# Paced loads, messages by SyncE while loads remain, and turns of queries, keys and w3 chunks on all rows of TensorE at once

## The chip, the cores and the metric

The kernel runs on one core of a Trainium2 chip. The metric is device time in microseconds (us) of one execution, lower is better. Each run is slow when it lies over 1.5% above the fastest of the same kernel, fast otherwise; fast runs are compared with fast runs. A core has five engines that each work through a program of their own: TensorE (PE in the profile; PEld is its weight loads), VectorE (DVE), ScalarE (ACT), GpSimd (POOL), SyncE (SP). They wait for each other through semaphores. A "q" behind a name (SPq, POOLq) is the engine's sequencer, which takes instructions in order and issues them.

## The reference

Block-sparse attention, then a gated feed-forward product, without a nonlinearity in it:

```python
# q, k, v: (4, 8, 768, 64); sampled_blocks: (24, 3)
scores = scale * np.matmul(q, k.transpose(0, 1, 3, 2))
scores = np.where(mask, scores, -1000000000.0)     # window, first and last block, sampled blocks
attn = softmax(scores)
attn_out = np.matmul(attn, v)                      # -> x: (3072, 512)
a = x @ w1; b = x @ w2                             # 512 x 1024
h = a * b @ w3                                     # 1024 x 1024
return h @ w_out                                   # 1024 x 512
```

The kernel first multiplies w3 by w_out (its "fold"), so that the last two products become one. To do that it needs w3 transposed; to compute scores it needs queries and keys transposed.

## The kernel before

A planner lays out the whole program ahead of time: every piece of work has an engine, a duration and what it depends on, and the program is emitted in the planned order. Most products contract over 128 rows and run as two halves of 64 rows, each in its own half of the array (a "lane"). Halves of different products run side by side, so that one lane fills the gaps of the other. Both halves of a product add into the same bank (a piece of the memory that TensorE writes), and the program lets the second start only when the first is done. That handshake is a "message": an empty instruction on SyncE or GpSimd, whichever the plan finds free, that waits for the first half's last matmul; the second half waits for it.

```python
def ordered(box, part, mm):
    if part == 0:
        box["upper"] = mm.ins
    elif "told" in box:
        tc.add_manual_dep(mm.ins, box.pop("told").name, SYNC, reason="this half may start")

def tell(box, eng):
    told = box["told"] = (nc.sync if eng == "SP" else nc.gpsimd).nop(nofuse=True).ins
    tc.add_manual_dep(told, box.pop("upper").name, SYNC, reason="the other half is done")
```

Turns on TensorE (transpositions as products with an identity) are made in halves too: 14 of queries or keys at six chunks, two at four (their other two chunks are turned on all rows already), and eight of w3 at eight chunks:

```python
def emit(part, lane, j):                       # in transposes(); fold_transpose() is alike
    c, rows = lo + j, HALF[lane]
    if part == 0 and j == 0:
        take_bank(box, "tp", [128, 1024], BF16)
    ordered(box, part, nc.tensor.transpose(
        box["p"][:, c * 128 + 64 * lane:c * 128 + 64 * lane + 64],
        nat_of[b, pr][rows, c].rearrange("p h d -> p (h d)"), ident[rows, rows]))
```

Queries and keys of batches 1 to 3 that are not turned on TensorE are turned by DMA, which SyncE issues in pairs:

```python
def turn(eng):                                 # in turned()
    t = QK[b, pr] = qkt.tile([128, 2, S], BF16, tag="qkt", name="qkt")
    for x in range(2):
        nc.sync.dma_start_transpose(out=t[:, x, :].rearrange("r (c p) -> r c p", c=C),
                                    in_=ns[x].rearrange("p c h d -> p (c h d)"))
```

All loads are issued by GpSimd, which also carries messages; a load is just that:

```python
def load(emit, us, deps=(), dur=0.7):
    op = plan.add(Op("POOL", dur, lambda eng: emit(), deps))
    op.dma = us
    return op
```

The softmax here doesn't subtract the row's maximum and nothing guards it: scores larger than these inputs give would overflow.

## Time and profile before

| | before |
|---|---|
| time, median of 3 runs | 253.03 us |
| span in the profile | 251.7 us |
| TensorE busy / idle in the span | 239.0 / 12.7 us |
| waits of TensorE for its own program ("issue" gaps, start to start), before 62 us / later | 5.96 / 0.85 us |
| idle from 70 to 240 us | 0.5 us |
| messages by SyncE / by GpSimd | 194 / 19 |

How to read it: TensorE is the bound, above all behind 70 us, and its only sizeable idle time is early. An "issue" gap (nothing in the profile ended it) is put down to the program's delivery because the six of 0.4 us or more behind 15 us all end at an instruction whose number is the same modulo 256, and the program comes in blocks of 256.

### The profile page before, as it was taken

How to read it: one execution, taken by the hardware profiler on the slowest of the kernel's cores; microseconds unless marked ns; L12 is line 12 of the kernel's file. 1: busy time of each engine (PE TensorE's matmuls, PEld its weight loads, DVE VectorE, ACT ScalarE, POOL GpSimd, SP SyncE). 2: the span in 40 equal slices, each digit the busy share in tenths (PEclk: the TensorE clock that was granted, in tenths of full speed). 3: DMA queues.
4: the chain of work that ended last, by engine and by line, in shares of the span. 5: the costliest groups of instructions: out<-in, count | busy, mean ns of one | idle time of the engine just before them, and what ended most of it. 6: DMA issues, size and time to landing. Idle time of an engine off the chain costs nothing.

```text
span 251.7 us, 10960 instructions
## 1 busy us (share of the span) xinstructions
PE 239.0 (95%) x4817; PEld 189.0 (75%) x4817; DVE 180.5 (72%) x311; ACT 180.1 (72%) x342; POOL 76.9 (31%) x116
## 2 busy tenths in 40 slices
PE   7889889699999999999999999999999999999994
PEld 3568767668878889788878788988898887666642
DVE  7752343497799987879888679878879787788331
ACT  6869677688899999889989898889999781000000
POOL 4934757794960400259165010000000000000000
PEclk9979999999999999999999999999999999999998
DMA  6999999999997950399999835001020031000044
GB/s 188 180 195 182 181 207 188 179 176 105 113 134 94 120 42 3 64 143 185 97 118 144 186 98 43 4 35 54 5 87 3 3 128 46 0 3 0 11 158 167
DMA packets 80082, 25.59 MB, mean 102 GB/s; under 512 B 70180, under 2 KB 75044, under 8 KB 80036
## 3 DMA queue, kind: packets, MB, share of 16 engines
q0 software_dynamic: 61968, 13.90, 60.9%
q1 hardware_dynamic: 18032, 11.01, 18.0%
q8 instruction: 37, 0.61, 1.0%
q14 instruction: 9, 0.07, 0.1%
q10 hardware_dynamic: 36, 0.00, 0.0%
HBM read 29.36 MB, written 6.29 MB: 142 GB/s over the span
## 4 chain that ended last, share of the span: by engine, by line
PE 91%; DMA 4%; issue 2%; POOL 1%; SPq 0%; ACT 0%
PE o L874 21%; PE pb L950 15%; PE po L950 15%; PE pa L950 15%; PE s L828 14%; PE wp L950 6%; DMA w<-in_moe_w_dram 3%; PE xp L920 2%; DMA raw<-in_k_dram 1%; PE w3p L963 1%; PE tp L715 1%; SPq L516 0%; POOL vn L649 0%; POOL w L682 0%; ACT ob L588 0%
## 5 line engine op out<-in xcount | busy, mean ns | idle before, releaser
L836 ACT ACTIVATE e<-s 128x512 bf16<-128x512 f32 x288 | 153.8, 613 | 24.3 <-PE s L828 20.7
L828 PE MATMUL s<-qkt 64*128 64x256 bf16 x576 | 94.8, 271 | 0.6 <-DVE qkt L588 0.6
L950 PE MATMUL pa<-x,w_sb 64*128 64x512 bf16 x384 | 87.3, 376 | 0.0
L950 PE MATMUL pb<-x,w_sb 64*128 64x512 bf16 x384 | 85.7, 376 | 0.2 <-SPq L608 0.2
L874 PE MATMUL o<-vt,e 64*128 64x65 bf16 x2304 | 79.7, 190 | 2.9 <-issue 1.9
L874 PEld LDWEIGHTS <-e 64*128 64x128 bf16 x2304 | 75.7, 94 | 6.5 <-issue 3.3
L842 DVE TENSOR_TENSOR e<-e,mask 128x1920 bf16<-128x1920 bf16 x60 | 69.0, 1151 | 7.5 <-ACT e L836 6.9
L950 PEld LDWEIGHTS <-w_sb 64*128 64x128 bf16 x768 | 59.1, 94 | 16.8 <-SPq L608 1.2
L950 PE MATMUL po<-wf_sb,h 64*128 64x512 bf16 (+1 forms) x400 | 65.0, 368 | 0.0
L828 PEld LDWEIGHTS <-qkt 64*128 64x128 bf16 x576 | 45.7, 94 | 8.3 <-DVE qkt L588 0.9
L1015 DVE TENSOR_TENSOR h<-pb,a 128x512 bf16<-128x512 f32 x48 | 33.0, 688 | 11.9 <-PE pb L950 8.6
L950 PEld LDWEIGHTS <-h 64*128 64x128 bf16 x400 | 30.0, 94 | 11.1 <-SPq L608 1.5
L950 PE MATMUL wp<-wo_sb,wt 64*128 64x512 bf16 x128 | 31.6, 377 | 0.0
L588 ACT COPY ob<-po 128x512 f32<-128x512 f32 x10 | 5.9, 588 | 31.4 <-PE po L950 31.2
L646 POOL DMA_DIRECT2D vt<-in_v_dram x16 | 13.0, 820 | 36.3 <-PE xp L920 17.1
L828 PE MATMUL s<-G,hot 64*128 64x256 bf16 x96 | 20.6, 282 | 0.5 <-issue 0.5
L905 DVE TENSOR_TENSOR xn<-o,rec 128x256 bf16<-128x256 f32 x48 | 19.7, 419 | 1.1
L902 DVE RECIPROCAL rec<-o 128x4 f32<-128x4 f32 x48 | 8.5, 179 | 16.6 <-PE o L874 15.6
L588 ACT CAST a<-pa 128x512 bf16<-128x512 f32 x23 | 13.7, 597 | 7.5 <-PE pa L950 7.4
L588 DVE CAST a<-pa 128x512 bf16<-128x512 f32 x25 | 17.2, 689 | 2.4 <-PE pa L950 1.9
L588 DVE COPY ob<-po 128x512 f32<-128x512 f32 (+1 forms) x15 | 9.7, 653 | 12.6 <-PE po L950 10.6
L760 POOL DMA_DIRECT2D nt<-in_q_dram x16 | 13.1, 821 | 14.3 <-PE s L828 8.6
(69 smaller groups left out, 183.8 us busy)
## 6 DMA issues: line engine op xcount, KB each, us to landing
out_dram<-ob SPq DMA_DIRECT2D x23, 256.0 KB, 2.1
w<-in_moe_w_dram POOLq DMA_DIRECT2D x8, 256.0 KB, 7.7
w_sb<-in_moe_w_dram POOLq DMA_DIRECT2D x8, 256.0 KB, 6.5
vn<-in_v_dram POOLq DMA_DIRECT2D x8, 192.0 KB, 7.9
nt<-in_q_dram POOLq DMA_DIRECT2D x16, 96.0 KB, 4.5
nt<-in_k_dram POOLq DMA_DIRECT2D x16, 96.0 KB, 5.0
vt<-in_v_dram POOLq DMA_DIRECT2D x16, 96.0 KB, 4.8
kn<-in_k_dram POOLq DMA_DIRECT2D x12, 96.0 KB, 7.3
```

What stands on the lines that cost most here:

```text
L588: (nc.scalar.copy if eng == "ACT" else nc.vector.tensor_copy)(dst, src)
L646: nc.gpsimd.dma_start(out=t[:, h, :, :D], in_=src[b][:, 2 * pr + h])
L760: nc.gpsimd.dma_start(out=n[:, :, h, :], in_=src[b][:, :, 2 * pr + h, :])
L828: nc.tensor.matmul(box["s"][:, k2 * QT:(k2 + 1) * QT], lhsT=hot[HALF[h], kc, :] if what else qk[HALF[h], 1, kc * 128:(kc + 1) * 128], rhs= ...
L836: nc.scalar.activation(E[key][:, g, :], box["s"], AF.Exp, scale=1.0 / 8.0)
L842: nc.vector.tensor_tensor(e, e, m.to_broadcast((128, 4, 4, 120)), op=ALU.mult)
L874: ordered(box, part, nc.tensor.matmul(box["p"][:, g, :], lhsT=E[es[kp]][HALF[lane], g, at:at + 128], rhs=VT[(4 * b + 2 * Q + i) % NV][HALF ...
L902: nc.vector.reciprocal(box["rec"], box["p"][:, :, D:])
L905: nc.vector.tensor_tensor(XN[key][:, 256 * Q:256 * Q + 256].rearrange("p (g d) -> p g d", g=4), box["p"][:, :, :D], box["rec"].to_broadcas ...
L920: ordered(box, part, nc.tensor.transpose(box["p"][:, c, at:at + 64], XN[b, t, qh][rows, 128 * c:128 * c + 128], ident[rows, rows]))
L950: ordered(box, part, nc.tensor.matmul(box["p"][:, :width], lhsT=lhsT[HALF[lane]], rhs=rhs[HALF[lane], cols], start=part == 0 and j == 0, s ...
L1015: nc.vector.tensor_tensor(h_of["h"][:, f, :], box["p"], a_of[f], op=ALU.mult)
```

## The change

Its intent, as far as the code tells: loads are held back so that only some 8 us of load is on its way at a time, which should let other traffic through, the instruction blocks among it. The turns run on all 128 rows at once, which halves their instruction count and needs no handshake. And while loads remain to be issued, every message goes by SyncE, because a GpSimd that waits for the pace of its loads cannot pass messages.

```diff
     def tell(box, eng):
-        told = box["told"] = (nc.sync if eng == "SP" else nc.gpsimd).nop(nofuse=True).ins
+        if "upper" not in box:
+            return
+        told = box["told"] = (nc.sync if eng == "SP" or left else nc.gpsimd).nop(nofuse=True).ins
@@
+    on_way, AHEAD, left = deque(), 8.0, []
+
     def load(emit, us, deps=(), dur=0.7):
-        op = plan.add(Op("POOL", dur, lambda eng: emit(), deps))
+        def issue(eng):
+            left.pop()
+            made = emit()
+            for dma in made:
+                ahead, behind = sum(t for _, t in on_way) + us / len(made), None
+                while on_way and ahead > AHEAD:
+                    behind, t = on_way.popleft()
+                    ahead -= t
+                if behind is not None:
+                    tc.add_manual_dep(dma.ins, behind.ins.name, SYNC, reason="few loads at a time")
+                on_way.append((dma, us / len(made)))
+        left.append(1)
+        op = plan.add(Op("POOL", dur, issue, deps))
@@ transposes()
         def emit(part, lane, j):
-            c, rows = lo + j, HALF[lane]
             if part == 0 and j == 0:
-                take_bank(box, "tp", [128, 1024], BF16)
-            ordered(box, part, nc.tensor.transpose(... [rows, c] ..., ident[rows, rows]))
+                for x in range(n):
+                    whole(0, 0, x)
@@ fold_transpose()
             if part == 0 and j == 0:
                 take_bank(box, "w3p", [128, NF, 128], BF16)
-            ordered(box, part, nc.tensor.transpose(... w3_sb[i][rows, ...], ident[rows, rows]))
+                for x in range(NF):
+                    nc.tensor.transpose(box["p"][:, x, :], w3_sb[i][:, x * 128:(x + 1) * 128], ident)
```

(Every load returns the DMAs that it made, and the output weights are loaded in four pieces instead of one.) The planner does not know of any of this: it still plans two halves for a turn and puts messages where it did; the emitted program differs from its plan.

## The prediction

> **What bounds the kernel now.** I read the page first, from the top down. TensorE's row:
>
> ```profile
> PE 239.0 (95%) x4817; PEld 189.0 (75%) x4817; DVE 180.5 (72%) x311; ACT 180.1 (72%) x342; POOL 76.9 (31%) x116
> PE   7889889699999999999999999999999999999994
> ```
>
> TensorE is busy for 95% of 251.7 us, and the digits show where it is not: the first nine slices, about 56 us. Then the stretches, in the view by windows (columns: stretch, its length, then busy time and count of PE, PEld, DVE, ACT, POOL, then clock, DMA share, GB/s):
>
> ```profile
> 0.00:60.00 60.00, 51.59 (x1116) 40.19 (x1116) 32.03 (x74) 45.19 (x86) 39.54 (x70) 0.97 1.44 185
> 70.00:150.00 80.00, 79.47 (x1757) 65.85 (x1756) 67.21 (x108) 73.04 (x143) 26.19 (x34) 1.00 1.05 109
> 150.00:240.00 90.00, 90.00 (x1630) 70.33 (x1627) 70.97 (x112) 52.51 (x100) 1.53 (x2) 1.00 0.13 35
> ```
>
> Up to 60 us TensorE idles 8.4 us beside a stream of loads at 185 GB/s. From 70 to 240 us it idles 0.5 us in 170: there TensorE sets the end, and a stall put into it is paid almost in full. The chain of waits, from 28 to 50 us, says what the early idle time is (start, length, what):
>
> ```profile
> 29.43 1.18 issue
> 36.43 0.87 issue
> 42.73 0.48 issue
> 47.63 2.06 issue
> ```
>
> "issue" means that nothing in the profile released TensorE. I counted its instructions (weight loads and matmuls alike) up to each of these gaps: they end at number 961, 1217, 1473 and 1729 (gaps of 1.36, 1.19, 0.75 and 2.25 us from start to start), then 0.40 at 2241 and 0.57 at 5825. All lie a multiple of 256 apart: TensorE waits for its own program. The page's queue list has that transfer:
>
> ```profile
> q8 instruction: 37, 0.61, 1.0%
> ```
>
> 37 packets of 16 KB, each 256 instructions. In the trace such a packet starts 1.9 to 4.3 us after TensorE enters a block in the loaded phase (mostly under 1.5 us after 80 us), takes 1 to 1.8 us, and the gap ends 1.5 us later: 5.2 to 6.7 us in all, while a block of early work lasts only 4 to 7 us. The loads themselves are not the early bound: the q and k tiles land 2 to 6 us before TensorE uses them at 25 to 33 us, and 8 to 10 us before at 50 to 69 us. Only the second w3 chunk, at 13.8 us, holds it up (1.5 us).
>
> Last, the handshakes. A product in two halves lets the second half start only when SyncE or GpSimd has passed a message. Two answers show who passes them and what else SyncE does:
>
> ```profile
> L608 SPq EVENT_SEMAPHORE  x194: 17/17/17, 6.9 to 246.5; - x194
> L608 POOLq EVENT_SEMAPHORE  x19: 17/17/17, 36.5 to 149.2; - x19
> L769 SPq DMA_TRANSPOSE qkt<-nt x16: 1210/1216/2022, 73.3 to 149.1; - x16
> ```
>
> 194 messages go by SyncE and 19 by GpSimd. SyncE also issues 16 DMA transposes, in eight pairs, and each holds it 1.2 us or more.
>
> **What the Trainium skill says.** "Runtime: NRT & Kernel Launch", section Instruction fetch mechanics: the program is streamed in 16 KiB blocks of 256 instructions by the sequencer's own DMA queue, mostly hidden, and TensorE's buffer holds 2048 instructions. The trace agrees on the blocks, not on the rest: six gaps, 6.5 us in sum, and a block is asked for only one block ahead. "DMA: Bandwidth & Descriptors", Queues, rings and completion order: an engine goes round its queues packet by packet. That fits a fetch that waits longer under load. "TensorEngine Tiling (Array Packing)", Key Properties: changing the tiling mode drains the array. In the trace, a 64-row weight load follows a 128x128 spare matmul 147 ns after its start, where 56 ns is the step between two such; the other way round 198 ns against 109. So about 90 ns a switch. "Perfetto Trace Analysis", DMA Instruction — HWDGE: the issuing sequencer is free only at the reported end. The trace agrees: a pair's second transpose, long ready, starts 0.12 us after the first ends.
>
> **The change part by part.** The built order of both programs shows that all matmuls but the turns keep their order (4501, equal one by one). What differs:
>
> 1. *Turns on all rows.* 312 half transposes become 156 whole ones: 312 TensorE instructions fewer, counting weight loads. Time: the halves took 7.8 us start to start without gaps over 100 ns (222 at some 32 ns, 81 woven into the other half's work at 10 ns). The wholes at the 56 ns step that the trace shows for a warm pair: 156 x 56 = 8.7 us. Switches: 24 items x 2 x 90 ns = 4.3 us at most. Sum +5.2 us; as some items lie side by side and the first seven fall where data is awaited anyhow, I count +4.
> 2. *Their handshakes.* 24 messages go. Gaps of 0.1 to 0.2 us ahead of second halves: 1.7 us by my count. -1.7.
> 3. *Instruction fetch.* With 312 fewer instructions before 70 us, block borders fall at other work. Placing them on before's timeline with its gaps taken out, the blocks last 6.4, 6.4, 6.1, 4.5, 6.1, 6.5 and 4.2 us where they lasted 6.2, 3.9, 6.7, 4.7, 5.7, 4.4 and 3.7. At some 6 us per fetch the short ones still stall, 2 to 3.5 us in sum where 5.95 were lost by 61 us. -3.
> 4. *Pacing.* The framework already keeps at most eight loads on their way (each issue waits for the eighth before). The new limit of 8 us of load binds for the 256 KB chunks (six of 1.27 us) and for the output weights, now in four pieces; runs of 96 KB pieces stay limited by the eight. The queue is first come, first served and never dry (loads land 5 to 13 us after issue), so landings don't move. It may shorten the fetch a little: 0 to -1, within the range.
> 5. *Messages moved.* While loads remain to be issued (the last at about 150 us), every message now goes by SyncE. All 19 of GpSimd lie before that. The first moved one of each cluster stands in SyncE's order just behind a pair of DMA transposes. The eight, with the start of the second half that needs it now, and the end of the pair:
>
> ```
> needed at   75.59  80.29  85.45  103.15  125.05  129.74  138.88  148.84
> pair ends   75.98  81.70  87.29  104.43  126.01  132.04  140.70  150.32
> stall (+.1)  0.5    1.5    1.9     1.4     1.1     2.4     1.9     1.6
> ```
>
> Sum 12.3 us. The pair starts right behind the message before it, as now, so it won't move ahead of TensorE. I take off 5% for work that catches up: +11.7.
>
> Sum: +4 - 1.7 - 3 + 11.7 = +11. From 253.0: 264; a little off for pacing gives **263.5 us**.
>
> **The rivals.** (a) *The early gain is all there is*: the moved messages come in time, the fetch gaps go, and the time is 247 to 250. For it: the gaps are real, and the author meant this. Against it: the eight pairs, whose ends lie behind the need in each case. It would hold if a transposing issue did not block SyncE. (b) *The stalls come but are made up*, because ScalarE gets ahead meanwhile: 255 to 259. Against it: from 70 us on TensorE has next to no idle time that a freer ScalarE could fill. (c) *Worse than the sum*: stalls of 2 us drop TensorE's clock. The gap at 12 to 13.8 us was followed by matmuls of 410 ns instead of 270, the one at 47.6 us by none: 266 to 270. (d) *Pacing starves the load stream*, and TensorE waits at 20 to 45 us: +1 to +4. Against it: six chunks, landing 1.25 us apart in the trace, cover 7.5 us, and the first load of all took 2.2 us from issue to landing.
>
> **Range and chances.** The stalls range from 9 (two missed, some made up) to 14 us (longer transposes); the early part from -4 to +3. So 257 to 269 holds it 8 times in 10. Faster by over 2% (under 248.0) needs (a) with all of the fetch gain: 0.04. Within 2% (to 258.1) needs (b) or a large early gain: 0.14. Slower: 0.82.
>
> **What would show it.** Right: messages on GpSimd gone; eight gaps of 0.5 to 2.4 us on TensorE between 73 and 155 us, put down to SyncE, each ending with a pair of transposes; PE idle time in that stretch near 12 us instead of 0.5; "issue" gaps before 61 us at 2 to 3.5 us; whole transposes at 56 ns; 60 us' worth of early work finishing within 2 us of before. Wrong: the stretch from 70 to 150 us as full as now (then SyncE is not held, or the messages are not needed there); or fetch gaps unchanged (then the count of instructions does not set them).

## The result, and the profile after

| | before | after |
|---|---|---|
| time, median (range), 4 runs each | 252.93 us (252.31 to 255.64) | 268.13 us (267.78 to 268.57) |
| span in the profile | 251.7 us | 266.4 us |
| TensorE busy / idle | 239.0 / 12.7 us | 249.5 / 16.9 us |
| "issue" gaps before 62 us / later | 5.96 / 0.85 us | 0 / 2.12 us |

The change made the kernel slower: ratio 1.058, 95% interval 1.050 to 1.066. (A ratio here is the mean time of one kernel's fast runs over that of the other's fast runs of the same rounds, so not quite the ratio of the medians.)

TensorE's row and slices on the page of the kernel after:

```profile
PE 249.5 (94%) x4661; PEld 190.5 (71%) x4661; DVE 181.4 (68%) x311; ACT 181.9 (68%) x342; POOL 78.7 (30%) x119
PE   8899999999987799899879698999999999999994
```

The idle slices have changed places: the early ones are full now, and there are 7s and a 6 in the middle. TensorE does more: 10.5 us more busy time with 156 matmuls fewer. The same three stretches as before, in the view by windows:

```profile
0.00:60.00 60.00, 58.13 (x1006) 42.16 (x1008) 32.97 (x77) 46.91 (x87) 43.52 (x76) 1.00 1.46 186
70.00:150.00 80.00, 71.01 (x1531) 57.30 (x1529) 62.02 (x98) 66.10 (x127) 26.11 (x33) 1.00 1.06 92
150.00:240.00 90.00, 87.57 (x1726) 70.82 (x1728) 68.79 (x110) 60.80 (x115) 0.00 (x0) 0.98 0.14 42
```

Up to 60 us TensorE is busy 58.1 us where it was 51.6, yet it has not got further: at equal points of the program (both programs hold the same 4501 matmuls besides the turns, in the same order) it is 0.95 us later at 72 us (a half of one lane may start a little before or after its neighbour of the other; the order within each lane is the same). So that busy time is not more work done. From 70 to 150 us it idles 9.0 us where it idled 0.5. The loads move 186 GB/s early, as before. The shares of the chain that ended last, before and then after:

```profile
PE 91%; DMA 4%; issue 2%; POOL 1%; SPq 0%; ACT 0%
```

```profile
PE 88%; SPq 4%; DMA 4%; issue 1%; ACT 1%; POOL 1%
```

SyncE's sequencer is new in it, with 4% of 266 us. One of its places in the chain of waits, from 82.67 us (start, length, what):

```profile
82.67 0.12 PE s L840
82.80 0.06 SPq L781
...
82.97 1.21 SPq L781
84.18 0.05 issue
84.23 0.02 SPq L610
84.25 0.05 issue
84.29 0.39 PE pa L962
```

L781 is the issue of a DMA transpose, L610 a message, L962 the second half of a feed-forward product. The data of that second half is not late: what it waits for is the message, the message stands behind a transpose that holds SyncE for 1.21 us, and 0.05 us after the transpose's end it is passed on. The answers on the two lines show the rest (count, then shortest, median and longest in ns, then first and last start), and that GpSimd passes no message any more:

```profile
L610 SPq EVENT_SEMAPHORE  x189: 17/17/17, 18.3 to 261.2; - x189
L781 SPq DMA_TRANSPOSE qkt<-nt x16: 1211/1228/1910, 74.3 to 162.3; - x16
```

The waits of TensorE for it, in the view of waits (us in sum, times, longest):

```profile
PEld L962 <- SPq L610: 10.4, 17, 2.1
PE o L886 <- SPq L610: 3.5, 2, 2.0
PE pa L962 <- SPq L610: 3.4, 3, 1.5
PE pb L962 <- SPq L610: 3.1, 2, 1.9
```

The three PE rows hold seven waits, 10.0 us. The eight places one by one: the gap between starts of matmuls, less the ordinary step there (up to 0.1 us), and how much further after lies behind before once it is past. At the fifth, no gap is ended by SyncE: TensorE waited 0.86 us for its own program at 131.7 us, just ahead of it, and what it lost there is put in brackets.

| pair of transposes ends at (us) | 77.6 | 84.2 | 91.4 | 110.0 | 132.7 | 139.1 | 151.1 | 163.5 | sum |
|---|---|---|---|---|---|---|---|---|---|
| stall that the prediction listed | 0.5 | 1.5 | 1.9 | 1.4 | 1.1 | 2.4 | 1.9 | 1.6 | 12.3 |
| gap on TensorE | 1.09 | 1.73 | 2.17 | 1.25 | (0.4) | 1.68 | 2.30 | 1.57 | 11.8 without the fifth |
| further behind at equal points | 1.12 | 1.68 | 1.75 | 1.22 | (0.41) | 1.75 | 2.29 | 1.39 | 11.6, 11.2 without it |

Between them, two late waits for the program, at 120.8 and 147.1 us, add 0.64 and 0.60 us, and 0.93 us is lost right behind the stall that ends at 151.2 us. There the granted clock (the share of its full clock that TensorE is allowed) was 0.50 from 151.8 us for 3.4 us, and a step between two products of one lane that took 0.21 us at 155.6 us took 0.43 us at 154.2 us. 0.95 + 11.61 + 0.64 + 0.60 + 0.93 = 14.7 us, the difference of the spans; it stays at 14.7 to the end: nothing is caught up.

What a turn costs is seen on the timeline of TensorE (start, length, then operation). Before, two turns in halves (tp and w3p) woven into the products of the other lane:

```profile
26.84 0.19 PE L874 MATMUL o<-vt,e 64*128 64x65 bf16 x1
26.87 0.19 PE L963 MATMUL w3p<-ident,w 64*128 64x64 bf16 x1
26.87 0.19 PE L874 MATMUL o<-vt,e 64*128 64x65 bf16 x1
26.90 0.19 PE L963 MATMUL w3p<-ident,w 64*128 64x64 bf16 x1
```

After, a whole turn between two products:

```profile
31.43 0.82 PE L962 MATMUL wp<-wo_sb,wt 64*128 64x512 bf16 x3
32.18 0.51 PE L735 MATMUL tp<-ident,qn 128*128 128x128 bf16 x6
32.62 0.39 PE L962 MATMUL wp<-wo_sb,wt 64*128 64x512 bf16 x1
```

Before, the half turn of w3 starts every 30 ns while the other lane goes on every 30 ns: it takes next to nothing from it. After, the six chunks take the whole array for 0.44 us (32.18 to 32.62). The trace has their starts 56 ns apart, so 6 x 56 = 0.34 us are the stream and 0.10 us the way back to halves; 0.31 us passed between the start of the last product ahead of them and theirs, where two such products start 0.22 us apart. So the way in and the way back took 0.09 + 0.10 us here.

### The profile page after: what moved, and what is told of

It is laid out like the page before. It is cut to its first block, busy times and chain, and to the rows that moved or that the text cites. A ratio compares the mean times of both kernels' runs of the same rounds, so it can differ in the third digit from the quotient of the medians.

```text
span 266.4 us, 10632 instructions
## 1 busy us (share of the span) xinstructions
PE 249.5 (94%) x4661; PEld 190.5 (71%) x4661; DVE 181.4 (68%) x311; ACT 181.9 (68%) x342; POOL 78.7 (30%) x119
## 4 chain that ended last, share of the span: by engine, by line
PE 88%; SPq 4%; DMA 4%; issue 1%; ACT 1%; POOL 1%
PE o L886 20%; PE pb L962 14%; PE pa L962 14%; PE s L840 14%; PE po L962 14%; PE wp L962 6%; SPq L781 4%; DMA w<-in_moe_w_dram 2%; PE tp L735 2%; PE w3p L975 2%; PE xp L932 2%; DMA raw<-in_k_dram 1%; ACT e L848 1%; SPq L516 0%; POOL vn L664 0%
## 5 line engine op out<-in xcount | busy, mean ns | idle before, releaser
L840 PE MATMUL s<-qkt 64*128 64x256 bf16 x576 | 93.5, 271 | 0.8 <-DVE qkt L588 0.7
L962 PE MATMUL pa<-x,w_sb 64*128 64x512 bf16 x384 | 87.2, 378 | 3.4 <-SPq L610 3.4
L962 PE MATMUL pb<-x,w_sb 64*128 64x512 bf16 x384 | 85.9, 379 | 3.1 <-SPq L610 3.1
L886 PE MATMUL o<-vt,e 64*128 64x65 bf16 x2304 | 81.1, 190 | 4.9 <-SPq L610 3.5
L854 DVE TENSOR_TENSOR e<-e,mask 128x1920 bf16<-128x1920 bf16 x60 | 69.1, 1151 | 12.7 <-ACT e L848 12.4
L962 PEld LDWEIGHTS <-w_sb 64*128 64x128 bf16 x768 | 59.3, 94 | 25.5 <-SPq L610 8.4
L962 PE MATMUL po<-wf_sb,h 64*128 64x512 bf16 (+1 forms) x400 | 66.5, 370 | 0.0
L840 PEld LDWEIGHTS <-qkt 64*128 64x128 bf16 x576 | 44.3, 94 | 10.5 <-DVE qkt L588 1.8
L1025 DVE TENSOR_TENSOR h<-pb,a 128x512 bf16<-128x512 f32 x48 | 33.1, 689 | 16.0 <-PE pb L962 12.7
L962 PEld LDWEIGHTS <-h 64*128 64x128 bf16 x400 | 30.1, 94 | 9.6 <-SPq L610 1.2
L962 PE MATMUL wp<-wo_sb,wt 64*128 64x512 bf16 x128 | 32.1, 378 | 0.1
L840 PE MATMUL s<-G,hot 64*128 64x256 bf16 x96 | 19.3, 269 | 0.0
L588 DVE COPY ob<-po 128x512 f32<-128x512 f32 (+1 forms) x15 | 9.7, 653 | 12.6 <-PE po L962 10.6
```

The costliest lines, as they stand in the source:

```text
L588: (nc.scalar.copy if eng == "ACT" else nc.vector.tensor_copy)(dst, src)
L840: nc.tensor.matmul(box["s"][:, k2 * QT:(k2 + 1) * QT], lhsT=hot[HALF[h], kc, :] if what else qk[HALF[h], 1, kc * 128:(kc + 1) * 128], rhs= ...
L854: nc.vector.tensor_tensor(e, e, m.to_broadcast((128, 4, 4, 120)), op=ALU.mult)
L886: ordered(box, part, nc.tensor.matmul(box["p"][:, g, :], lhsT=E[es[kp]][HALF[lane], g, at:at + 128], rhs=VT[(4 * b + 2 * Q + i) % NV][HALF ...
L962: ordered(box, part, nc.tensor.matmul(box["p"][:, :width], lhsT=lhsT[HALF[lane]], rhs=rhs[HALF[lane], cols], start=part == 0 and j == 0, s ...
L1025: nc.vector.tensor_tensor(h_of["h"][:, f, :], box["p"], a_of[f], op=ALU.mult)
```

## The experiments

The change has three parts that can be had alone: pacing (P), whole turns (W), messages by SyncE (S). All kernels below gave correct results. Chips and calls differ by up to 1% in the time of the kernel before (medians 252.9 to 255.8 us), so each ratio is against the kernel before on its own chip. This table sums up the parts; busy and idle are TensorE's, from the page of each.

| kernel | parts | ratio (95%) | span | busy | idle | "issue" gaps before 62 us / later |
|---|---|---|---|---|---|---|
| before | - | 1 | 251.7 | 239.0 | 12.7 | 5.96 / 0.85 |
| pace_only | P | 0.998 (0.993 to 1.003) | 252.7 | 240.8 | 11.9 | 4.09 / 2.07 |
| whole_only | W | 1.006 (1.001 to 1.012) | 255.1 | 246.3 | 8.8 | 0 / 0.69 |
| planned_msgs | P W | 1.005 (1.000 to 1.011) | 256.2 | 245.6 | 10.6 | 0 / 2.02 |
| sp_alone | S | 1.031 (1.024 to 1.039) | 262.8 | 239.9 | 22.9 | 6.51 / 0.28 |
| whole_sp | W S | 1.057 (1.048 to 1.065) | 265.9 | 249.0 | 16.9 | 0 / 1.34 |
| after | P W S | 1.058 (1.050 to 1.066) | 266.4 | 249.5 | 16.9 | 0 / 2.12 |

**planned_msgs: the change, with messages as planned.** The theory was that moved messages carry nearly all of the loss; the rival, that whole turns or pacing cost something of that size themselves.

```diff
-        told = box["told"] = (nc.sync if eng == "SP" or left else nc.gpsimd).nop(nofuse=True).ins
+        told = box["told"] = (nc.sync if eng == "SP" else nc.gpsimd).nop(nofuse=True).ins
```

> The changed kernel, but the messages between halves go by SyncE or GpSimd as the plan has them (19 by GpSimd again). Theory A (the moved messages wait behind pairs of DMA transposes): the eight stalls of 0.4 to 2.3 us, 11.6 us in sum at equal places of the program, go, and 255 to 257 us are left. Theory B (the whole turns, with their changes of tiling mode, cost the time): it stays at 264 us or more. Theory C (paced loads come too late): it stays too, with waits on loads.

Measured: 257.38 us (256.74 to 257.92) against 255.82, ratio 1.005: just above the 255 to 257 us expected of the theory, and far from the rivals' 264. The stretch from 70 to 150 us of this kernel:

```profile
70.00:150.00 80.00, 76.07 (x1695) 63.60 (x1693) 64.93 (x104) 70.52 (x136) 24.54 (x31) 1.00 1.01 101
```

TensorE is busy for 76.1 us of it, against 71.0 with all parts; the gaps of the table above are gone. What is left are two waits for SyncE of 1.03 and 1.59 us, behind transposes that took 2.3 to 2.6 us in this run, and late waits for the program. So the moved messages are 10.2 us of span (266.4 to 256.2). The rest of the change is 4.5 us by the spans of two profiles from different chips, but half a per cent (1.3 us) by the ratio, which compares on one chip. The spans of the kernel before lie between 252.1 and 254.9 us in this call, so the size of the rest is known no better than that.

**sp_alone: the kernel before, with all messages by SyncE.** This is the suspected part alone, without anything that the rest could contribute.

```diff
-        told = box["told"] = (nc.sync if eng == "SP" else nc.gpsimd).nop(nofuse=True).ins
+        told = box["told"] = nc.sync.nop(nofuse=True).ins
```

> The kernel before with one edit: all messages by SyncE. Theory A: 264 to 266 us, with eight gaps of TensorE that end with a pair of transposes, 11 to 12 us in sum. Theories B and C: 252.5 to 254 us, as turns and loads are those of before.

Measured: 264.64 us (261.93 to 266.16) against 255.82, ratio 1.031. The same stretch:

```profile
70.00:150.00 80.00, 71.51 (x1571) 57.85 (x1566) 61.80 (x98) 65.93 (x127) 28.45 (x36) 1.00 1.21 100
```

8.5 us idle, as in the kernel after. The eight gaps are there: 0.52, 1.31, 2.54, 1.21, 1.32, 1.65, 1.68 and 1.57 us, 11.8 in sum, and at equal points this kernel falls 11.1 us behind the kernel before, as its span does. By its times it lost only 8.8 us; the kernel before was some 3 us slower than usual on that chip, and nothing that I ran tells why the two did not move together. The stalls are caused by the messages on SyncE alone, in either reading.

**pace_only: the kernel before, with the pacing.** Turns in halves, messages as planned.

```diff
 # the kernel after, with both turns as in the kernel before, and
-        ... (nc.sync if eng == "SP" or left else nc.gpsimd) ...
+        ... (nc.sync if eng == "SP" else nc.gpsimd) ...
```

> The kernel before with the loads paced and nothing else (turns in halves, messages as planned). If pacing shortens the instruction fetch by itself: gaps marked issue before 61 us under 2 us instead of 5.95, and 247 to 250 us. If the smaller count of instructions closed those gaps: 4 us of them or more stay, and 252 to 254 us. Theory C: waits on loads appear and 254 us or more.

Measured: 255.25 us (254.46 to 256.03) against 255.82, ratio 0.998. The early waits for the program fall from 5.96 to 4.09 us, and later ones rise from 0.85 to 2.07 us. The loads move 184 GB/s in the first 60 us, against 185. Eight us of load ahead is enough to keep the stream as full as before, and no gain shows. The 4 us that are left are what was expected if pacing by itself does not shorten the fetch.

**whole_only: whole turns without a limit on loads.** Messages as planned.

```diff
-    on_way, AHEAD, left = deque(), 8.0, []
+    on_way, AHEAD, left = deque(), 1e9, []
```

> The kernel before with the turns on all rows alone (no limit on loads, though the output weights come in four pieces; messages as planned). By my sum the turns cost 4 us and give back 1.7 of handshakes and 3 of fetch: 252 to 254 us. From the changed kernel's trace (1 us behind at 72 us with no fetch gap left) the turns cost 8 to 9 rather than 4: then 255 to 259 us, depending on the fetch gaps that stay without pacing. Theory B: 264 us or more.

Measured: 257.02 us (256.68 to 258.96), ratio 1.006. No wait for the program before 62 us. Its row on the page:

```profile
PE 246.3 (97%) x4661; PEld 190.1 (75%) x4661; DVE 181.0 (71%) x311; ACT 180.9 (71%) x342; POOL 79.0 (31%) x119
```

TensorE is busy 7.3 us longer than before (246.3 to 239.0) and idle 3.9 us less. Here the two sides of the early part can be read: the fetch waits are gone, and in their place the array is occupied for some 7 us more, as the second of the two expectations had it. At equal points it is 1.2 us behind at 72 us.

**touch: only the switch of modes.** One whole transpose of the item's first chunk ahead of each of the 24 half items, overwritten by the halves. It measures the disputed cost, that of leaving the half mode and coming back to it, while halves and handshakes stay. It also adds 48 instructions, where the change takes 312 away.

```diff
                 take_bank(box, "tp", [128, 1024], BF16)
+                nc.tensor.transpose(box["p"][:, lo * 128:lo * 128 + 128],
+                                    nat_of[b, pr][:, lo].rearrange("p h d -> p (h d)"), ident)
             ordered(box, part, nc.tensor.transpose(
@@ and in fold_transpose() before its halves
+                nc.tensor.transpose(box["p"][:, 0, :], w3_sb[i][:, :128], ident)
```

> The kernel before, with one whole-array transpose (its result is overwritten) put ahead of each of the 24 half-turn items: 24 x 56 ns = 1.3 us of streaming, and the same 48 changes of tiling mode that the whole turns bring. Theory D (a change of mode empties both halves of the array: some 0.26 us an item, as I read it from the changed kernel's trace): TensorE is 6 to 8 us later at 72 us than in the kernel before, and the time 2 to 3% longer. Theory E (the changes of mode are cheap; the whole turns cost because the halves were woven into other work for nothing): under 2.5 us later, within 1%.

Measured: 257.5 us (256.68 to 258.71) against 253.67, ratio 1.016. Its row on the page:

```profile
PE 248.6 (98%) x4841; PEld 194.0 (76%) x4841; DVE 181.3 (71%) x311; ACT 181.2 (71%) x342; POOL 77.2 (30%) x116
```

9.6 us more busy time than before, for 24 chunks that stream in 24 x 56 ns = 1.3 us. The other 8.3 us are 0.35 us an item: an estimate, since busy spans are partly modelled. Counted otherwise, as 2.9 us further behind plus 5.25 us of vanished fetch waits less the stream, it is 0.29 us. Neither theory's range was met: 3 us later at 72 us and 1.6% lie between D and E; it is with the vanished waits added that D's cost comes out. Both counts take in all else that differs between the two executions: behind its wait at 13.8 us the kernel before ran at a granted clock of 0.50 from 14.9 us for 3.4 us, and touch did not. A third count leaves that out: how much further behind touch is right after a visit than right before it. For the twelve visits behind 20 us that lie clear of before's fetch waits the median is 0.29 us with the stream, or 0.23 us without. So a visit of the whole array among halves costs 0.2 to 0.35 us besides its stream, by estimate.

The surprise is the waits for the program: 0.71 us of 5.96 are left, though this program is longer than before. So the waits do not vanish because there are fewer instructions. What fits is that TensorE waits when the work of a block lasts less than its successor takes to come. The trace has the packets of that transfer, so both can be read (a block counted from where TensorE enters it, waits included; a fetch to the landing of the packet, plus the 1.5 us after which the waits ended):

| blocks entered between 25 and 57 us | 1 | 2 | 3 | 4 | 5 | 6 |
|---|---|---|---|---|---|---|
| before: block / fetch, us | 5.2 / 5.2 | 6.7 / 6.7 | 5.9 / 5.9 | 6.5 / 6.4 | 6.7 / 5.8 | 4.0 / 4.0 |
| touch: block / fetch, us | 4.7 / 4.8 | 6.8 / 7.0 | 4.8 / 3.7 | 5.7 / 3.4 | 6.6 / 5.7 | 4.8 / 4.5 |

In before, five of six blocks last just as long as the fetch. In touch, longer work is one half of the story (without its wait of 2.25 us, before's fourth block is 4.2 us of work, against 5.7); the other is that two fetches came 2.2 and 3.0 us sooner, for which no run has the cause. Fetch waits and added work fill the same time: of the 9.6 us of added busy time here, idle time gave 6.5 (12.7 to 6.2 us), and the span grew by 3.1.

**w3_whole_pace: a smaller share of whole turns.** Pacing, and only the eight turns of w3 whole, which have eight chunks per switch; messages as planned. If the fetch gain and the switches could be had in a better proportion, this would be a version that beats before.

```diff
 # the kernel after, with messages as planned and, in transposes(),
-                for x in range(n):
-                    whole(0, 0, x)
+            # ... the halves of the kernel before
```

> Paced loads (8 us), the eight w3 items whole, queries and keys in halves, messages as planned. With some 0.26 us a change-over and 8 x 8 x 56 ns the eight items should cost 3 us more than in halves; 128 instructions fewer should close two of the early fetch gaps, about 2 us. So within 1% of paced loads alone (ratio 0.99 to 1.01 to the kernel before). Were the changes of mode cheap: 0.98 to 0.99.

Measured: 254.58 us (252.66 to 256.34), ratio 1.005 (0.995 to 1.015). It is 1.46 us ahead of before at 72 us, and 0.11 us ahead at the end, by a wait of 1.36 us behind a transpose and later waits for the program. No gain that the rounds can see, as the expectation had it.

**pace5 and pace4: the pace tightened to 5 and to 4 us of load.** Halves, messages as planned. This asked where pacing begins to starve TensorE, and whether a thinner stream lets the program through.

```diff
-    on_way, AHEAD, left = deque(), 8.0, []
+    on_way, AHEAD, left = deque(), 5.0, []      # 4.0 in pace4
```

> Paced loads alone, but 5 us of load on their way instead of 8 (turns in halves, messages as planned). If the fetch waits behind the loads in flight, its early gaps fall below the 4.1 us seen with 8 us, to 1 to 3 us, and the time to 250.5 to 254 us on a chip where the kernel before takes 255.8 (ratio 0.98 to 0.995). If loads come too late: waits on loads appear and the ratio is over 1.00.

> As the run with 5 us, with 4 us on their way: three chunks of 256 KB. Fetch gaps under 1.5 us if they follow the loads in flight; but three chunks cover under 4 us of a path that takes over 2 us from issue to landing, so the load stream may show holes, and TensorE waits on loads before 45 us. Ratio 0.98 to 1.02, no more than a guess.

Measured: pace5 268.9 us, ratio 1.057 (1.047 to 1.067); pace4 280.3 us, ratio 1.106 (1.099 to 1.113). In pace5 the second of the expected cases came, loads too late and a ratio over 1.00; for pace4 the guess of 0.98 to 1.02 missed. Of the five early waits for the program, four are gone in pace5; the fifth, 0.41 us at 60 us in before, is 1.39 us and comes at 70 us, as this kernel is late by then. And the stream of loads falls to 152 GB/s in the first 60 us (138 in pace4). The view of waits of pace5, longest first among TensorE's:

```profile
PE o L889 <- POOLq L610: 7.4, 1, 7.4
...
PE pa L965 <- POOLq L610: 2.1, 1, 2.1
```

One wait of 7.4 us for a message on GpSimd. The chain of waits in that stretch shows what GpSimd was at:

```profile
39.23 3.83 DMA w_sb<-in_moe_w_dram
43.06 1.57 issue
44.63 1.47 POOL kn L667 x2
46.10 0.48 issue
46.58 0.02 POOLq L610
```

The message (L610) stands behind loads that wait for an earlier load to land. That is what the change moved its messages to SyncE for: the rule in it cures a fault of the pacing, one that at 8 us of load did not show.

**pace5_early_sp: the same, with messages by SyncE only until the first DMA transpose.** If that reading is right, the stall goes without a new one behind transposes.

```diff
+    turns = []                                  # turn() appends to it
-        ... (nc.sync if eng == "SP" else nc.gpsimd) ...
+        ... (nc.sync if eng == "SP" or not turns else nc.gpsimd) ...
```

> The kernel with halves and loads paced at 5 us, but messages go by SyncE until the first pair of DMA transposes has been issued (about 73 us), and as planned after it. Theory (messages on GpSimd stand behind loads that wait for their pace, and that is why the change sent them by SyncE): the stall of 7.6 us at 47 us, ended by a message on GpSimd, is gone; the waits on q and k loads at 27 to 34 us (3.9 us in sum) and the stall of 2.2 us at 87 us stay: ratio 1.02 to 1.035, some 7 us under the kernel paced at 5. Rival (the pace itself starves TensorE, and the message only happens to end the wait): the same stall is ended by a load instead, ratio 1.045 or more.

Measured: 269.64 us (266.58 to 271.04) against 255.36, ratio 1.064 (1.055 to 1.073). The total went against me (1.02 to 1.035 was expected). Its waits:

```profile
PE pa L966 <- POOLq L610: 6.8, 1, 6.8
PE tp L730 <- DMA qn<-in_q_dram: 4.1, 3, 2.5
PE w3p L979 <- DMA w<-in_moe_w_dram: 1.8, 2, 1.6
```

The stall at 47 us is gone, and at equal points the gain is what was foretold: at 74 us this kernel is 3.1 us behind before, where pace5 is 9.9 us behind. TensorE still waits on loads in that stretch, but the waits for its program, 5.55 us in before by 50 us, are gone, and at 50 us this kernel is 1.3 us ahead of before. The total missed its range because the same stall comes back. Once messages go by GpSimd again, one waits 7.0 us behind paced loads (to 85.7 us; 2.2 us at this place in pace5), and behind it another 1.4 us is lost while the granted clock is 0.50 (from 81.5 us for 6.8 us). The rival has a smaller share: the 3.1 us, or 4.5 us against pace_only, which is 1.4 us ahead of before there, are what the pace of 5 us costs by itself. Neither defect shows at 8 us.

**pace7_early_sp and pace7_again: the attempt at a version that beats both.** The same with 7 us of load ahead, run twice because most of its times were called slow.

```diff
-    on_way, AHEAD, left, turns = deque(), 5.0, [], []
+    on_way, AHEAD, left, turns = deque(), 7.0, [], []
```

> The same with 7 us of load ahead: a version that could beat both, if a shorter queue of loads lets the instruction fetch come sooner without starving TensorE. For that: fetch gaps before 62 us under 3 us (pacing at 8 us left 4.1 of 6.0), no load waits over 0.5 us, ratio 0.985 to 0.995. Against it (pacing moves only the fetch's luck): ratio 0.995 to 1.01, and gaps in another place.

> The same kernel again (halves, loads paced at 7 us, messages by SyncE until the first pair of DMA transposes), in more rounds, because three of its four times were called slow and one was 251.15 us. If it is a version that beats both, its ratio is under 0.99 with the interval below 1. If the one fast time was chance, the ratio is 0.995 to 1.005 and the interval holds 1.

Measured: 255.3 us (251.15 to 257.84, one fast run of four, so no ratio), then 256.55 us (251.38 to 258.77, two fast of six), ratio of the fast ones 0.994 (0.986 to 1.002). The profiles fell in the slow state; both show the waits for the program as they were (5.5 and 6.9 us before 62 us). The interval holds 1 and the medians are no better: not a gain that can be claimed. No version that I ran is clear of the kernel before.

**whole_sp: the change without its pacing.** Whole turns and messages by SyncE; the last corner of the table.

```diff
-    on_way, AHEAD, left = deque(), 8.0, []
+    on_way, AHEAD, left = deque(), 1e9, []
```

> The change without its pacing: whole turns, and all messages by SyncE while loads remain; the output weights still come in four pieces, as in the other kernels without the change's limit. Theory (the pace at 8 us moves nothing; stalls behind DMA transposes and the cost of mode switches make the difference): ratio 1.05 to 1.066, as the whole change, with the eight stalls of 10.5 to 12.5 us in sum. Rival (part of the 15 us comes from loads that are held back): ratio 1.03 to 1.045.

Measured: 267.3 us (266.34 to 269.25) against 254.24, ratio 1.057 (1.048 to 1.065), with seven gaps ended by SyncE of 11.6 us in sum. Two of its waits, to set beside those of the kernel after:

```profile
PE o L886 <- SPq L610: 3.2, 2, 1.9
PE pa L962 <- SPq L610: 3.5, 3, 1.4
```

As expected; the pacing has no part in the loss that these intervals can see. Here too the fifth pair has no gap of its own, and a stretch of 3.4 us at a granted clock of 0.50 follows a stall, at 92.6 us.

## Why the prediction was right or wrong

The time was foretold at 263.5 us and is 268.1, inside the range but near its upper end; the direction and the main cause were right. Step by step:

- *Messages moved, +11.7.* Right in cause and in size: seven of the eight stalls came, listed at 11.2 us in sum and found at 11.8 as gaps, 11.2 as distance that is lost. The eighth, listed at 1.1, was taken up by a wait for the program that cost 0.41. The 5% taken off for catching up was wrong in reason: nothing was caught up. sp_alone shows the cause by itself, planned_msgs its absence. The sign "idle time near 12 us" between 73 and 155 us reads 10.2, as the last stall falls at 163 us.
- *Turns on all rows, +4, and handshakes, -1.7.* The net of the two was +2.3 and is about +7: by busy time in whole_only 7.3 us, by distance 0.95 us behind at 72 us plus the 5.96 us of fetch waits that vanished = 6.9 us. (Both are low by some 1.0 us, which before alone lost at half clock from 14.9 us on.) The step of 56 ns was right. The switches, put at 2 x 90 ns an item, are 0.19 us in the example above and 0.2 to 0.35 us in touch, so they were mis-sized by a factor of two at most. More lies in the halves, counted as 7.8 us of TensorE's time: woven into the other lane they took less than their own stream. The distance before and behind the whole turns says so too: in whole_only the twelve items behind 20 us that lie clear of before's fetch waits cost 0.55 us more than their halves in the median, about the whole stream (six chunks, 0.34 us) and a visit.
- *Instruction fetch, -3.* It was -6 early, and some +1.3 later (2.12 us behind 62 us instead of 0.85). The prediction set lengths of blocks by instruction count against "some 6 us per fetch", and both were off. Its lengths in before are misread for four of seven blocks: with the waits taken out the trace gives 6.2, 3.8, 5.5, 5.2, 4.2, 6.7 and 3.6 us (the same sum). In the kernel after, the blocks entered from 25 to 54 us lasted 7.9, 5.4, 6.8, 8.0 and 5.5 us, as the whole turns in them took longer than counted, and the fetches 5.4, 3.5, 4.5, 5.8 and 3.4. touch, with 48 instructions more than before, has 0.71 us of early waits left, so their count does not decide. A part of the early gain is the turns' own slowness, and the terms for turns and fetch were not to be added as if apart; that the errors in them, +4.7 and -3, largely cancel is luck.
- *Pacing, 0 to -1.* Right as far as can be seen: 0.998 alone, and no difference between whole_sp and after. That it did nothing because the stream stays full was the reason given, and 184 to 186 GB/s in the kernels that pace at 8 us (185 before) agrees.
- *What was missing from the sum*: 0.93 us at half clock behind the stall at 151 us, and the late waits for the program.
- *The rivals.* (a), only the gain: refuted by the seven gaps. (b), made up later: refuted by the constant 14.7 us. (c), a falling clock: true behind one of the seven stalls, for 0.93 us (granted clock 0.50 for 3.4 us); behind the others the clock stayed, the one of 2.17 us included. It named 266 to 270, where the time fell, but not for its reason. (d), starved loads: refuted at 8 us, true at 5 and 4.

Open is why sp_alone lost 11.1 us by its profile and 8.8 us by its median against the kernel before on the same chip; the spread of the kernel before (252.9 to 255.8 us) is of that size.

## What to carry to other kernels

A message that takes 17 ns to send can cost as much as what stands ahead of it in its engine's order (here up to 2.3 us, behind pairs of issues of 1.2 us or more): before moving a handshake to another engine, list what that engine issues just before each place. Work that a plan weaves into another's gaps can be nearly free, so count a change of its form by what it displaces, not by its own stream. And a wait that ends because something else got slower is not a gain: compare the two at equal points of the program, not by the busy share.

## What the Trainium skill lacked or had wrong

- "Runtime: NRT & Kernel Launch", Instruction fetch mechanics, calls the crossing of a block "mostly hidden" and gives TensorE a buffer of 2048 instructions. The blocks of 256 agree, and so does its word that the next page is fetched while the current one runs (the prediction counts this among what does not agree). Otherwise the measurement decides: 5.96 us of waits in the first 62 us of the kernel before and 0.85 us later, at block borders only, and no sign of a buffer of more than the next block. The page gives no time for a fetch: here 4.0 to 6.7 us from entering a block in that stretch, against 3.6 to 6.7 us of work in one.
- "TensorEngine Tiling (Array Packing)", Key Properties, says that changing the tiling mode drains the array, and gives no cost. Here a visit of 128-row work among 64-row work cost 0.2 to 0.35 us besides its stream (touch, three ways of counting), and 0.09 + 0.10 us ahead of it and behind it in the example shown. That it is the draining that takes this time is not shown.
- "Perfetto Trace Analysis", DMA Instruction — HWDGE, says rightly that the sequencer is free at the reported end of the issue. It gives no duration for a transposing issue: 1.21 to 1.91 us in the kernel after, up to 2.6 us in planned_msgs. What no page that I read spells out is the consequence for handshakes on that engine: 11.8 us in seven stalls.
- "DMA: Bandwidth & Descriptors", Queues, rings and completion order, describes how engines share their time among queues. That would suggest that fewer loads on their way let a fetch through sooner. With 8 us of load on its way the early waits were 4.1 us, with 7 us 5.5 and 6.9 us, with 5 us 1.4 us (at the same places). The fetches of the six blocks above took 5.7 us in the mean in before, 5.3 with 8 us of load on its way and 4.6 with 5 us, but 4.4 us (five of them) in whole_only, where nothing is held back; that a thinner stream alone speeds the fetch is not shown.
